# A chunked state recurrence on TensorE: 40 weight columns for the state product, and the state part of u in four 64x64 quarters

## The chip, the cores and the metric

The kernel runs on one core of a Trainium2 chip. The engines named below are PE (TensorE, matrix products; its weight loads are shown as PEld), DVE (VectorE), ACT (ScalarE), POOL (GpSimd) and SP (SyncE, which issues most DMAs). The metric is the time of one execution on the device in microseconds. Three executions of the kernel before took 243.11, 243.59 and 246.12 us; the median is 243.59 us.

## The reference

There are 4 x 8 = 32 heads, 768 time steps and a head width of 40. Each head keeps a 40 x 40 state, and a row of all heads' outputs goes through two dense layers with a squared ReLU between them:

```python
y[:, :, t] = np.einsum('bhd,bhde->bhe', rt, state)
Sa = np.einsum('bhde,bhe->bhd', state, at)
state_decay = state * wt[:, :, None, :] - np.einsum('bhd,bhe->bhde', Sa, bt)
state = state_decay + np.einsum('bhd,bhe->bhde', vt, kt)
...
h = x @ w_in            # x: 3072 x 320, w_in: 320 x 2048
r = np.maximum(h, 0.0)
return (r * r) @ w_out  # w_out: 2048 x 320
```

## The kernel before, in words

Time is cut into 12 chunks of 64 steps. Inside a chunk the recurrence is written as matrix products; the state is carried from chunk to chunk. The 32 heads are 16 pairs (p = 0..7 in each of two groups g = 0, 1; q = 0, 1 is the member of a pair). Heads are stored with 40 numbers in a field of 64, so that a pair fills 128 partitions.

A named step of the plan is a group of instructions on one engine. Those that matter here, for chunk c:

- `AS c` (line 743, PE): the state's part of u, the a rows times the old state. `AR` holds the scaled a for 128 partitions (64 for q = 0, 64 for q = 1); `STb` holds the old state with q = 0 in the upper 64 partitions and q = 1 in the lower 64, each in its own 40 columns and zeros in the other's. One matmul does both heads of a pair: 128 rows, 64 weight columns, 80 moving columns; 16 matmuls, mode "C" (two column halves of the array, by g).
- `EV c` (line 757, PE): adds to the same PSUM tile the part of u from this chunk's v; 32 matmuls of 40 moving columns with masked products `EN` as weights. In chunks 3 to 11 (`EVC`) it has 128 rows and mode "C".
- `u0 c` (ACT or DVE): copies u negated to `NZ`. `NU c` (line 772, PE): 32 matmuls with `EN` as weights and `NZ` moving, mode "Q" (64 rows by 64 columns, two of the four quarters). `u1 c` (ACT or DVE, lines 388 and 385): writes the sum into the `VU` buffer.
- `SC c` (line 793, PE): carries the old state into the new state's PSUM tile, 4 matmuls of 320 columns. `S c g0`, `S c g1` (line 805, PE): adds the products of k and b (`KB`, the weights, 64 columns of which 40 are used) with v and u (`VU`, 40 moving columns); 32 matmuls in a chunk, mode "C". `s c` (line 808, DVE): scales the sum into `STb`.
- `RS c` and `Y c` (PE): the same for the output y, one chunk behind. `EN`, `CX`, `TA`, `TR`, `TK`, `TV`, `TS`, `XT`, `cf`, `ci`: products, transposes and running sums of a chunk, each of many small matmuls. `F`, `FL` and `O`: the dense layers, 128 x 128 weights with 256 or 320 moving columns.

Every matmul has its own weight load, so that PE's program has two instructions for each. All matmuls are issued by a helper at line 402, transposes at 406 and 409.

The order of all instructions on all engines is written out by hand as a text (`ORDER`, lines 87 to 212) and issued as it stands: dense layers of earlier chunks stand between the small groups of later ones. The costs that the steps carry (`d` in `pe`, lines 344 to 349) don't reorder anything when the kernel is built. The class that holds the plan has among its constants:

```python
LAT = {"PE": 235, "ACT": 70, "DVE": 70, "POOL": 80, "SP": 100}
SWITCH = 110
LINE, FETCH = 256, 4350
```

`SC` and `S` are left out in the last chunk, which needs no new state.

Of the kernel before, what the change touches and what calls it, by code (L numbers as in the profile page):

```python
# [7 lines left out]
FP32 = mybir.dt.float32  # L8
# [211 lines left out]
def kernel(  # L220
# [13 lines left out]
    NB, NHH, T, D = r.shape  # L234
# [3 lines left out]
    NJ = NH // 2  # L238
    NP = NJ // 2
# [11 lines left out]
    def rows(g):  # L251
        return slice(64 * g, 64 * g + 64)
# [25 lines left out]
    EVC = range(3, 12)  # L278
# [65 lines left out]
    def pe(name, mode, cols, mms, **kw):  # L344

        d = {"R": max(28.6, cols / 2.4 + 1) / 2, "Q": max(31.0, cols / 2.4 + 1) / 2,
             "C": max(31.0, cols / 2.4 + 1) / 2,
             "D": max(22 if cols < 64 else 60.6, cols / 2.4 + 2.5)}[mode]
        plan.add(name, [("PE", d * len(mms))], ("pe", d, mms), mode=mode, n_mm=len(mms), **kw)
# [51 lines left out]
    def mm(o_, l_, r_, start, stop):  # L401
        return lambda: nc.tensor.matmul(out=o_(), lhsT=l_(), rhs=r_(), start=start, stop=stop,  # L402
                                        skip_group_check=True)
# [320 lines left out]
    def rec(c):  # L724
        KBK = [("KB", c % NK, 0), ("KB", c % NK, 1)]
        q2 = c % 2
        n = NP * D
        kb, vu = KB[c % NK], VU[c % NK]
        VU0 = [("VU0", c % NK, 0), ("VU0", c % NK, 1)]
        hb = ("U", c)  # L730

        def uo(p, g, q, w_=1):
            j = 2 * p + q
            return lambda: slot(hb, FP32)[rows(g), j // NP,
                                          D * (j % NP):D * (j % NP) + D * w_]
        ms = []
        if c > 0:
            for p in range(NP):
                for g in range(2):
                    ms.append(mm(uo(p, g, 0, 2), lambda p=p, g=g: AR[q2][:, 0, g, p, :],  # L740
                                 lambda p=p, g=g: STb[(c - 1) % 2][:, NP * g + p, :, 0:D],
                                 p % 4 == 0, False))
            pe(f"AS {c}", "C", 80, ms, reads=[("AR", q2, 0), ("AR", q2, 1), ("STb", (c - 1) % 2, 0),
                                             ("STb", (c - 1) % 2, 1)],
               writes=[hb], alloc=[hb])
        ms = []
        for p in range(NP):
            for q in range(2):
                for g in range(2):
                    ms.append(mm(uo(p, g, q),  # L750
                                 lambda p=p, q=q, g=g: (EN[q2][:, g, q, p, :] if c in EVC else
                                                        EN[q2][rows(1 - g), g, q, p, :]),
                                 lambda p=p, q=q, g=g: vu[:, NJ * g + 2 * p + q, 0:D]
                                 if c in EVC else vu[rows(1 - g), NJ * g + 2 * p + q, 0:D],
                                 c == 0 and p % 4 == 0 and q == 0, False))
        VU1 = [("VU1", c % NK, 0), ("VU1", c % NK, 1)]
        pe(f"EV {c}", "C" if c in EVC else "Q", 40, ms,
           reads=both(("EN", q2, 0), ("EN", q2, 1)) + VU0 + (VU1 if c in EVC else []),
           writes=[hb], alloc=[hb] if c == 0 else [])
        ew(f"u0 {c}", copy_alts(  # L760
            lambda: NZ[0][:].rearrange("p (s j) e -> p s (j e)", s=2),
            lambda: slot(hb, FP32)[:, :, 0:n], 2 * n, scale=-1.0),
           reads=[hb], writes=[("NZ",)])
        ms = []
        for p in range(NP):
            for q in range(2):
                for g in range(2):
                    ms.append(mm(uo(p, g, q),
                                 lambda p=p, q=q, g=g: EN[q2][rows(g), g, q, p, :],
                                 lambda p=p, q=q, g=g: NZ[0][rows(g), 2 * p + q, :],  # L770
                                 False, True))
        pe(f"NU {c}", "Q", 40, ms, reads=both(("EN", q2, 0), ("EN", q2, 1)) + [("NZ",)],
           writes=[hb])
        for g in range(2):
            ew(f"u1 {c} g{g}", copy_alts(
                lambda g=g: vu[rows(g), NJ * g:NJ * g + NJ, 0:D].rearrange(
                    "p (s j) e -> p s j e", s=2),
                lambda g=g: slot(hb, FP32)[rows(g), :, 0:n].rearrange(
                    "p s (j e) -> p s j e", e=D), 2 * n, scale=-1.0),
               reads=[hb], writes=[("VU1", c % NK, g), ("bank", hb)], free=[hb])  # L780
        if c < NCH - 1:
            hs = ("S", c)
            if c > 0:
                ms = []
                for g in range(2):
                    for q in range(2):
                        ms.append(mm(
                            lambda q=q, g=g: slot(hs, FP32)[rows(q), g, 0:n].rearrange(
                                "p (i e) -> p i e", e=D),
                            lambda q=q: IDQ[:, rows(q)],  # L790
                            lambda q=q, g=g: STb[(c - 1) % 2][:, NP * g:NP * g + NP, q, 0:D],
                            True, False))
                pe(f"SC {c}", "C", n, ms, reads=[("STb", (c - 1) % 2, 0),
                                                ("STb", (c - 1) % 2, 1)],
                   writes=[hs], alloc=[hs])
            for g in range(2):
                ms = []
                for p in range(NP):
                    for q in range(2):
                        ms.append(mm(  # L800
                            lambda p=p, q=q, g=g: slot(hs, FP32)[rows(q), g, D * p:D * p + D],
                            lambda p=p, q=q, g=g: kb[:, NJ * g + 2 * p + q, :],
                            lambda p=p, q=q, g=g: vu[:, NJ * g + 2 * p + q, 0:D],
                            c == 0 and p == 0, True))
                pe(f"S {c} g{g}", "C", 40, ms, reads=KBK + [VU0[g], VU1[g]] + [hs] * g,
                   writes=[hs], alloc=[hs] if c == 0 and g == 0 else [])
            for q in range(2):
                ew(f"s {c} q{q}", [("DVE", c_dve(2 * n), lambda q=q: nc.vector.tensor_tensor(  # L808
                    out=STb[q2][rows(q), :, q, 0:D],
                    in0=slot(hs, FP32)[rows(q), :, 0:n].rearrange("p g (i e) -> p g i e", e=D),  # L810
                    in1=GT[c % NG][rows(q), :, L:L + 1].broadcast_to([64, NJ, D]),
                    op=ALU.mult))],
                   reads=[hs, ("GT", c % NG)], writes=[("STb", q2, q)], free=[hs])
            if c in DTS:
                turn(f"dS {c}", lambda: Sb[q2][:].rearrange("p i q e -> p i (q e)"),
                     lambda: STb[q2][:].rearrange("p i q e -> p (i q e)"),
                     [("STb", q2, 0), ("STb", q2, 1)], [("Sb", q2)])
                return
            ht = ("A", "TS", c)
            ms = []  # L820
            for pi in range(NJ):
                for q in range(2):
                    ms.append(tp(
                        lambda pi=pi, q=q: slot(ht, BF16)[:, q, 64 * pi:64 * pi + 64],
                        lambda pi=pi, q=q: STb[q2][rows(q), pi].rearrange("p x e -> p (x e)"),
                        q))
            if c in WHOLE:
                ms = [tpw(lambda pi=pi, ht=ht: pairs_at(ht, pi),
                          lambda pi=pi: STb[q2][:, pi].rearrange("p x e -> p (x e)"))
                      for pi in range(NJ)]  # L830
            pe(f"TS {c}", *tmode(c), ms, reads=[("STb", q2, 0), ("STb", q2, 1)], writes=[ht],
               alloc=[ht])
            ew(f"tS {c}", copy_alts(
                lambda: Sb[q2][:, :, :, 0:D] if c in WHOLE else Sb[q2][:, :, :, 0:D].rearrange(
                    "p i q e -> p q i e"),
                lambda: (slot(ht, BF16)[:].rearrange("p h (m q e) -> p (h m) q e", q=2, e=64)
                         if c in WHOLE else slot(ht, BF16)[:].rearrange(
                             "p q (i e) -> p q i e", e=64))[:, :, :, 0:D],
                1280, True),
               reads=[ht], writes=[("Sb", q2)], free=[ht])  # L840
# [283 lines left out]
```

## Time and profile before

| | |
|---|---|
| median of three executions | 243.59 us |
| span of the profiled execution, first to last instruction | 241.4 us |
| PE busy | 219.8 us (91%) |
| PE weight loads busy | 173.8 us (72%) |
| DVE, ACT, POOL busy | 185.1, 171.9, 119.3 us |
| matmuls, and as many weight loads | 5360 |

The profiled execution is given by its span alone, without what lies around it; the median is 2.2 us above that span. The page of the profile has the busy time of each engine, the span in 40 slices, the DMA queues, the chain of work that ended last, and the costliest groups of instructions. In a timeline row stand the start, the length, the engine, the line, the operation with its operands and shapes, and the count of instructions merged into the row; a name such as `pb<-STb,AR` is output <- moving operand, weights. Lengths of matmuls are modelled and overlap, so the pace of a group is read from the start of one group to the start of the next.

### The profile page before, as it was taken

Reading aid. Unit: us, or ns where it says so; the run is one execution under the profiler, and the core shown is the slowest. Engines: PE = TensorE matmul, PEld = TensorE weight load, DVE = VectorE, ACT = ScalarE, POOL = GpSimd, SP = SyncE. Lnnn points to the kernel's source line nnn. Section 1 sums busy time; section 2 is a strip of 40 time slices with the busy share of each in tenths; the row PEclk is TensorE's granted clock in tenths of the full one; section 3 lists DMA queues with packets and bytes.
Section 4 is the critical chain, followed back from the end, with each engine's and each line's share of the span. In section 5 each row is a group of like instructions: output and inputs, shape, how many; then the busy total and the mean of one; then the engine's idle time right before and its main releaser. Section 6 shows DMA issues by size and latency. Waiting matters only on the chain.

```text
span 241.4 us, 11825 instructions
## 1 busy us (share of the span) xinstructions
PE 219.8 (91%) x5360; PEld 173.8 (72%) x5360; DVE 185.1 (77%) x237; ACT 171.9 (71%) x225; POOL 119.3 (49%) x117
## 2 busy tenths in 40 slices
PE   0569877999999999999999999999999999999992
PEld 0357666778887787777777877877787777877872
DVE  3779994889988898899789978779888668646430
ACT  3383876879699888976979995975897974572330
POOL 6237816403545572849948379318591750024330
PEclk9967997999999999999999999999999999999998
DMA  6989999997979987888783878978994857093413
GB/s 154 233 185 231 186 217 162 187 203 156 181 158 236 187 163 148 144 194 152 157 169 67 168 178 161 220 157 144 146 188 120 156 106 93 3 161 72 109 24 86
DMA packets 116808, 37.20 MB, mean 154 GB/s; under 512 B 103575, under 2 KB 116375, under 8 KB 116503
## 3 DMA queue, kind: packets, MB, share of 16 engines
q1 hardware_dynamic: 115574, 36.13, 75.7%
q8 instruction: 42, 0.69, 1.2%
q10 hardware_dynamic: 1184, 0.33, 0.6%
q14 instruction: 8, 0.06, 0.1%
HBM read 28.84 MB, written 3.93 MB: 136 GB/s over the span
## 4 chain that ended last, share of the span: by engine, by line
PE 74%; DMA 8%; SPq 7%; DVE 4%; ACT 3%; issue 2%; POOL 1%; POOLq 0%; ACTq 0%
PE pb L402 65%; PE pb L406 6%; DMA G<-in_moe_w_in_dram 4%; PE pb L409 3%; DMA osb<-in_moe_w_out_dram 2%; SPq L433 2%; SPq L1048 2%; DMA raw_w<-in_w_dram 2%; SPq L425 1%; DVE AR L682 1%; POOL WIN L392 1%; SPq L465 1%; DVE VU L385 1%; ACT lnW L548 1%; ACT VU L388 1%
## 5 line engine op out<-in xcount | busy, mean ns | idle before, releaser
L402 PE MATMUL pb<-WOUT,G 128*128 128x320 bf16 (+1 forms) x400 | 57.0, 294 | 0.1
L973 POOL TENSOR_TENSOR G<-G 128x1024 bf16<-128x1024 bf16 x22 | 41.8, 1910 | 28.4 <-ACT G L965 23.4
L402 PE MATMUL pb<-XT,WIN 128*128 128x256 bf16 x384 | 48.3, 273 | 0.0
L402 PEld LDWEIGHTS <-G 128*128 128x128 bf16 x400 | 36.4, 98 | 13.8 <-issue 0.5
L965 ACT ACTIVATE G<-pb 128x1024 bf16<-128x1024 f32 x36 | 36.0, 1021 | 11.1 <-PE pb L402 9.6
L402 PEld LDWEIGHTS <-WIN 128*128 128x128 bf16 x384 | 34.7, 98 | 8.0 <-issue 3.7
L713 DVE TENSOR_TENSOR EN<-pb,MSK 128x1024 bf16<-128x1024 f32 x24 | 28.8, 1216 | 4.9 <-PE pb L402 4.8
L713 DVE TENSOR_TENSOR CX<-pb,MSKI 128x1024 bf16<-128x1024 f32 x24 | 28.7, 1218 | 3.5 <-PE pb L402 3.2
L396 POOL TENSOR_TENSOR KB<-raw_kb,iG 128x640 bf16<-128x640 f32 x10 | 15.8, 1580 | 16.7 <-ACT iG L584 14.9
L808 DVE TENSOR_TENSOR STb<-pb,GT 64x640 bf16<-64x640 f32 x22 | 18.1, 821 | 3.4 <-PE pb L402 3.0
L392 POOL CAST VU<-raw_v 64x640 bf16<-64x640 f32 x17 | 13.3, 785 | 13.3 <-DMA raw_v<-in_v_dram 12.8
L896 DVE TENSOR_TENSOR Yb<-pb,Gin 128x128 bf16<-128x128 f32 (+1 forms) x24 | 12.3, 553 | 9.5 <-PE pb L402 9.4
L590 ACT ACTIVATE Gin<-pb 64x320 f32<-64x320 f32 x36 | 15.4, 428 | 4.6 <-PE pb L402 4.2
L396 POOL TENSOR_TENSOR lo<-lnW,hi 128x640 bf16<-128x640 f32 x7 | 9.8, 1402 | 16.4 <-DVE hi L383 16.2
L402 PE MATMUL pb<-XT,WLAST 64*128 64x256 bf16 x192 | 17.1, 271 | 0.0
L682 DVE TENSOR_TENSOR AR<-pb,GT 128x512 bf16<-128x512 bf16 x24 | 15.9, 683 | 1.6 <-PE pb L406 1.4
L402 PEld LDWEIGHTS <-EN 64*64 64x64 bf16 (+1 forms) x768 | 14.5, 111 | 3.4 <-issue 2.2
L388 ACT ACTIVATE VU<-pb 64x640 bf16<-64x640 f32 x17 | 11.8, 697 | 7.1 <-PE pb L402 4.0
L967 DVE TENSOR_SCALAR G<-pb 128x1024 bf16<-128x1024 f32 x12 | 14.4, 1212 | 1.8 <-PE pb L402 1.8
L388 ACT ACTIVATE VUT<-pb 128x2048 bf16<-128x2048 bf16 x6 | 11.3, 1876 | 5.4 <-PE pb L406 3.1
L402 PE MATMUL pb<-UTI,hi 64*128 64x64 bf16 x192 | 8.2, 198 | 7.3 <-POOL hi L392 6.9
L584 ACT ACTIVATE iG<-pb 128x640 f32<-128x640 f32 x18 | 12.6, 700 | 2.7 <-PE pb L402 2.1
(117 smaller groups left out, 442.7 us busy)
## 6 DMA issues: line engine op xcount, KB each, us to landing
raw_kb<-in_b_dram SPq DMA_DIRECT2D x24, 160.0 KB
raw_kb<-in_k_dram SPq DMA_DIRECT2D x24, 160.0 KB
raw_a<-in_a_dram SPq DMA_DIRECT2D x24, 160.0 KB
raw_v<-in_v_dram SPq DMA_DIRECT2D x24, 160.0 KB
raw_w<-in_w_dram SPq DMA_DIRECT2D x23, 160.0 KB
raw_r<-in_r_dram SPq DMA_DIRECT2D x22, 160.0 KB
out_dram<-osb SPq DMA_DIRECT2D x22, 160.0 KB
osb<-in_moe_w_out_dram SPq DMA_DIRECT2D x8, 320.0 KB
```

Of the source, the lines that this page charges most:

```text
L388: alts.append(("ACT", c_act(n), lambda: nc.scalar.activation(out=o_(), in_=i_(), func=ACTF.Copy, scale=1.0 if scale is None else scale)))
L392: lambda: nc.gpsimd.tensor_copy(out=o_(), in_=i_())))
L396: return [("POOL", 40 + 2.35 * n, lambda: nc.gpsimd.tensor_tensor(out=o_(), in0=a_(), in1=b_(), op=op)), ("DVE", c_dve(n), lambda: nc.vect ...
L402: return lambda: nc.tensor.matmul(out=o_(), lhsT=l_(), rhs=r_(), start=start, stop=stop, skip_group_check=True)
L406: return lambda: nc.tensor.transpose(out=o_(), in_=i_(), identity=IDb[rows(g), :])
L590: nc.scalar.activation(out=Gin[c % NGI][rows(g), NP * jh:NP * jh + NP, :].rearrange("p j e -> p (j e)"), in_=slot(hb, FP32)[rows(g), g, 0: ...
L682: ew(f"tA {c} g{g}", [("DVE", c_dve(512), lambda g=g: nc.vector.tensor_tensor(out=steps(AR[q2][:, 0, g]), in0=turned(ha, g), in1=steps(GT[ ...
L713: evac(f"m{nm} {c} g{g}", lambda s, n: [("DVE", c_dve(n), lambda: nc.vector.tensor_tensor(out=dst[q2][:, g, s].rearrange("p q i t -> p (q ...
L808: ew(f"s {c} q{q}", [("DVE", c_dve(2 * n), lambda q=q: nc.vector.tensor_tensor(out=STb[q2][rows(q), :, q, 0:D], in0=slot(hs, FP32)[rows(q) ...
L965: ("ACT", c_act(1024), lambda gb=gb, hf=hf: nc.scalar.activation(out=gb, in_=slot(hf, FP32)[:], func=ACTF.Relu)),
L967: ("DVE", c_dve(1024), lambda gb=gb, hf=hf: nc.vector.tensor_scalar(out=gb, in0=slot(hf, FP32)[:], scalar1=0.0, scalar2=None, op0=ALU.max))],
L973: ("POOL", 1900, lambda gv=gv: nc.gpsimd.tensor_tensor(out=gv, in0=gv, in1=gv, op=ALU.mult)),
```

## The change

Two edits, both in `rec(c)`; the text of the order stays as it is.

1. `S c` loads 40 weight columns in place of 64 and writes 40 PSUM partitions of each half in place of 64, in chunks 1 to 11 as far as they have the step (1 to 10). Chunk 0, which starts the PSUM tile, keeps 64.
2. In chunks 3 to 11, `AS c` has 32 matmuls in place of 16: each multiplies 64 rows (one q) by 64 weight columns (one g) with 40 moving columns, so that its four kinds use the four 64x64 quarters of the array. The two row halves write two PSUM banks: u's tile has bank q in place of the bank of pair half `j // NP`. `EV`, `NU`, `NZ` and the copy `u1` follow that layout. The mode of the step is "Q" in place of "C"; `EV` stays "C".

PE's program has 10,722 instructions before and 11,010 after: 9 chunks x 16 further matmuls and 16 further weight loads.

```diff
         def uo(p, g, q, w_=1):
+            if c in EVC:
+                return lambda: slot(hb, FP32)[rows(g), q, D * p:D * p + D]
             j = 2 * p + q
...
+        def uz(p, q):
+            return NP * q + p if c in EVC else 2 * p + q
...
-                    ms.append(mm(uo(p, g, 0, 2), lambda p=p, g=g: AR[q2][:, 0, g, p, :],
-                                 lambda p=p, g=g: STb[(c - 1) % 2][:, NP * g + p, :, 0:D],
-                                 p % 4 == 0, False))
-            pe(f"AS {c}", "C", 80, ms, reads=[("AR", q2, 0), ("AR", q2, 1), ("STb", (c - 1) % 2, 0),
+                    if c not in EVC:
+                        ms.append(mm(uo(p, g, 0, 2), lambda p=p, g=g: AR[q2][:, 0, g, p, :],
+                                     lambda p=p, g=g: STb[(c - 1) % 2][:, NP * g + p, :, 0:D],
+                                     p % 4 == 0, False))
+                        continue
+                    for q in range(2):
+                        ms.append(mm(uo(p, g, q), lambda p=p, g=g, q=q: AR[q2][rows(q), 0, g, p, :],
+                                     lambda p=p, g=g, q=q: STb[(c - 1) % 2][
+                                         rows(q), NP * g + p, q, 0:D], p == 0, False))
+            pe(f"AS {c}", *(("Q", 40) if c in EVC else ("C", 80)), ms, reads=[("AR", q2, 0), ("AR", q2, 1), ("STb", (c - 1) % 2, 0),
...
-                                 lambda p=p, q=q, g=g: NZ[0][rows(g), 2 * p + q, :],
+                                 lambda p=p, q=q, g=g: NZ[0][rows(g), uz(p, q), :],
...
-                    "p (s j) e -> p s j e", s=2),
+                    "p (j s) e -> p s j e" if c in EVC else "p (s j) e -> p s j e", s=2),
...
-                            lambda p=p, q=q, g=g: slot(hs, FP32)[rows(q), g, D * p:D * p + D],
-                            lambda p=p, q=q, g=g: kb[:, NJ * g + 2 * p + q, :],
+                            lambda p=p, q=q, g=g: slot(hs, FP32)[
+                                64 * q:64 * q + (D if c else 64), g, D * p:D * p + D],
+                            lambda p=p, q=q, g=g: kb[:, NJ * g + 2 * p + q, 0:D if c else 64],
```

## The prediction

> **What bounds the kernel now.** I read the page first: shares of the engines, the instruction queue and the chain that ended last.
>
> ```profile
> span 241.4 us, 11825 instructions
> PE 219.8 (91%) x5360; PEld 173.8 (72%) x5360; DVE 185.1 (77%) x237; ACT 171.9 (71%) x225; POOL 119.3 (49%) x117
> PE   0569877999999999999999999999999999999992
> q8 instruction: 42, 0.69, 1.2%
> PE 74%; DMA 8%; SPq 7%; DVE 4%; ACT 3%; issue 2%; POOL 1%; POOLq 0%; ACTq 0%
> ```
>
> PE is full from the tenth slice on (about 55 us) and makes up 74% of the chain; before that, loads end last. So PE time is worth its full size in chunks 3 and later, and about nothing before. The queue row matters below: 42 packets, 0.69 MB, 16 KB each. PE's program has 10,722 instructions, which is 42 blocks of 256.
>
> Second, PE's timeline around one chunk, for the pace of a group: start of the group to start of the next.
>
> ```profile
> 105.65 0.48 PE L402 MATMUL pb<-STb,AR 128*64 128x80 bf16 x16
> 105.96 0.66 PE L402 MATMUL pb<-VU,EN 128*64 128x40 bf16 x32
> 106.47 0.46 PE L402 MATMUL pb<-Sb,AR 128*64 128x80 bf16 x16
> 106.75 0.66 PE L402 MATMUL pb<-KB,CX 128*64 128x40 bf16 x32
> 107.35 0.41 PE L406 MATMUL pb<-IDb,tA 64*128 64x64 bf16 x16
> 107.69 0.68 PE L402 MATMUL pb<-NZ,EN 64*64 64x40 bf16 x32
> 108.30 2.35 PE L402 MATMUL pb<-WOUT,G 128*128 128x320 bf16 x16
> ...
> 112.13 0.46 PE L402 MATMUL pb<-STb,IDQ 128*64 128x320 bf16 x4
> 112.43 0.66 PE L402 MATMUL pb<-VU,KB 128*64 128x40 bf16 x32
> 113.02 1.05 PE L402 MATMUL pb<-XT,WIN 128*128 128x256 bf16 x8
> ```
>
> These are AS 5, EV 5, RS 4, Y 4, TA 6, NU 5, O 2, and SC 5, S 5, a dense group. EV, followed by a group of its own shape: 0.51 us for 32, 15.9 ns each. RS: 0.28 for 16. Y, the twin of EV but followed by another array shape: 0.60. So a change of shape costs 0.09 us. NU has 0.61 = 0.51 + 0.10: two quarters at 15.9 ns, and a change. AS takes 0.31, S 0.59 = 0.50 + 0.09.
>
> Third, where PE stops although it waits for no engine.
>
> ```profile
> 172.44 0.25 PE L402 MATMUL pb<-KB,CX 128*64 128x40 bf16 x5
> 172.85 0.59 PE L402 MATMUL pb<-KB,CX 128*64 128x40 bf16 x27 [0.17 <-issue]
> 173.38 1.05 PE L402 MATMUL pb<-XT,WIN 128*128 128x256 bf16 x8
> ...
> 202.05 0.64 PE L402 MATMUL pb<-AR,KBT 64*128 64x64 bf16 x31
> 203.10 0.19 PE L402 MATMUL pb<-AR,KBT 64*128 64x64 bf16 x1 [0.41 <-issue]
> ```
>
> Both stops fall inside a group. The first group needs 0.94 us to its successor instead of Y's 0.60: 0.34 lost. In the second, 31 of 32 matmuls take 1.05 us; at two for some 30 ns they need 0.48: 0.57 lost. Together 0.9 us. What lies between stops is shown by the windows (length, then PE busy and matmuls, PEld busy and weight loads, DVE, ACT, POOL):
>
> ```profile
> 32.28:37.93 5.65, 3.67 (x128) 3.41 (x128) 3.77 (x4) 4.93 (x7) 1.83 (x2) 1.00 1.06 246
> 106.78:172.85 66.07, 65.76 (x1801) 50.80 (x1796) 56.84 (x72) 51.63 (x71) 44.57 (x34) 1.00 0.81 154
> 167.81:172.85 5.04, 4.88 (x137) 3.53 (x134) 4.78 (x6) 3.73 (x8) 2.90 (x3) 1.00 1.12 106
> 172.85:203.10 30.25, 29.76 (x767) 23.46 (x767) 22.55 (x28) 24.11 (x34) 15.05 (x13) 1.00 0.79 149
> 199.04:203.10 4.06, 3.65 (x140) 2.92 (x135) 3.20 (x5) 1.10 (x3) 0.00 (x0) 1.00 1.14 134
> 65.82:70.01 4.19, 4.19 (x138) 3.60 (x134) 3.78 (x7) 3.78 (x7) 2.29 (x2) 1.00 0.63 118
> 172.85:177.16 4.31, 4.31 (x128) 3.46 (x128) 2.58 (x5) 3.61 (x7) 3.09 (x3) 1.00 0.97 203
> ```
>
> 32.28 and 37.93 are two earlier stops: exactly 128 + 128 = 256 instructions apart. 172.85 and 203.10 are 1534 counted instructions apart, six blocks of 256 with two that aren't counted. **The stops sit at block boundaries: PE waits for its next 256 instructions.** One block seems to be fetched while the one before it runs, so a block can't pass faster than a fetch. Stalled blocks took 4.06, 5.04 and 5.65 us; the one of 4.06 holds only 3.49 of work. The shortest unstalled ones here are 4.19 and 4.31. (A window cut in full flow also counts a dozen instructions still running.) I take 3.8 us as the floor of a block: between 3.49, which was too short, and 4.06, where one was held; the ends I keep are 3.4 and 4.06, with 5.0 for a single slow fetch.
>
> **The change part by part.**
>
> *S with 40 weight columns.* S runs at EV's 15.9 ns a matmul, RS with twice the moving columns at 17.5, so the 64-column weight load sets the pace of S, not its 40 moving columns. Bounds: nothing gained (15.9), or half of RS's pace for 80 columns (8.8). In proportion to columns it would be 9.9; I take 12, since small matmuls show no pace near that: 32 x 3.9 ns = 0.12 us a chunk. Eight of the ten chunks (3 to 10) lie where PE is full: **-1.0 us**, ends 0 and -1.8.
> [...]
>
> *AS in four quarters.* 32 matmuls. If each quarter keeps the 31.8 ns a matmul of EV and NU, four at once take 8 ns each: 0.25, and 0.03 for starting after another shape (AS 0.31 against RS 0.28). EV behind it keeps mode "C", so a change of shape is new: 0.09. That makes 0.37 against 0.31, x 9 chunks = **+0.5 us**. The trace shows no group with four quarters. Ends: 4.6 ns each, if only moving columns counted (-0.3 us), and 15.9, if four are no faster than NU's two: 0.61 against 0.31, +2.7 us.
>
> *Layout of u, NZ, VU.*
>
> ```profile
> L388 ACT ACTIVATE VU<-pb 64x640 bf16<-64x640 f32 x17 | 11.8, 697 | 7.1 <-PE pb L402 4.0
> ```
>
> The same counts and sizes on PE, ACT and DVE; the copy u1 writes runs of 40 as before. I cost it at nothing. It is covered by the dense groups that stand between NU and S; without that cover 5% of a copy of 0.7 us in 9 chunks would be 0.3 us.
>
> *Block boundaries.* Each quartered AS adds 32 instructions, so from chunk 3 on every boundary falls 32, 64, 96... instructions earlier in the same order. The boundary of 106.78 (14 blocks before 172.85) stands two matmuls into Y 4; after AS 3, 4 and 5 it stands 96 instructions earlier: 2 matmuls of Y, 16 of RS, 30 of EV, that is at 105.99. I carried all boundaries over in this way. Most new blocks need over 4 us. These, in the old times, don't (with the long block ahead of the third):
>
> ```profile
> 86.58:90.07 3.49, 3.49 (x121) 3.09 (x120) 3.10 (x5) 3.20 (x6) 2.69 (x3) 1.00 0.97 185
> 105.99:108.58 2.59, 2.59 (x138) 2.40 (x133) 2.41 (x5) 1.38 (x3) 2.05 (x2) 1.00 0.90 167
> 112.90:119.31 6.41, 6.41 (x133) 4.51 (x128) 6.33 (x7) 5.58 (x6) 6.14 (x6) 1.00 0.74 145
> 119.31:121.39 2.08, 2.08 (x126) 2.05 (x125) 0.50 (x2) 2.00 (x3) 2.08 (x2) 1.00 1.05 181
> 135.91:139.29 3.38, 3.38 (x126) 2.77 (x118) 2.80 (x4) 3.31 (x5) 1.01 (x2) 1.00 0.76 145
> 155.05:158.82 3.77, 3.77 (x134) 3.01 (x130) 2.96 (x4) 2.96 (x5) 0.00 (x0) 1.00 0.82 187
> ```
>
> The second is EV 5 to NU 5, 256 instructions with no dense matmul but three. The one from 119.31 is most of AS 6, RS 5, EV 6, Y 5 and cf 7. The block 199.04:203.10 stays where it is, with 3.49 of work, less 0.12 by S 10. Against 3.8 us they lack 0.3 + 1.2 + 1.7 + 0.4 + 0.0 + 0.4 = **+4.0 us** of new stops. The old two are gone or counted in: **-0.9 us**. Nothing hides a stop: PE is full after 55 us, with hardly a wait to take it back from. Floors of 3.4 and 4.06 give 1.6 and 5.9; a fetch of 5 us in one of the other blocks adds up to 1.
>
> *Sum:* -1.0 + 0.5 + 4.0 - 0.9 = +2.6: span 241.4 to 244.0; by the same step the median goes from 243.59 to **246.2 us** (+1.1%).
>
> **The rivals.**
>
> 1. *Fetches keep up.* If more than one block is held ahead, or a fetch begins earlier when dense matmuls stand queued, short blocks pass after long ones, as they do here (the 2.08 block follows one of 6.41). Then 243.59 - 1.0 + 0.5 - 0.9 + about 1 for what remains = 243.2; with both products at their best ends and no stop left, 240.6. Against it: the block of 3.49 that ends at 203.10 was held. [...] The 0.17 and 0.41 us of "issue" above speak against it in this trace.
> 2. *Slower by over 2%: the quarters don't run four at a time.* NU's two quarters go at exactly the pace of two column halves; if that pace is the issue of load and matmul pairs rather than the loads in a quarter, AS costs 0.61. The place is AS in nine chunks, the price +2.7 instead of +0.5. Its blocks then last 0.24 longer, so at a floor of 3.8 the stops are 3.4: 247.8. At 4.06 they are 5.0: 249.4. It passes 248.5 from a floor of about 3.9. For it: no faster pair than this stands in the rows above. Against it: a pair of RS moves 80 columns in 35 ns while another runs beside it, so the halves do overlap.
> 3. *The narrow load gains nothing*, as 40 columns still occupy a 64-column half: S stays at 0.59, 1.0 more than the forecast: 247.2.
>
> **How the numbers follow.** Forecast 246.2: 0.50. Fetches keep up (243.2): 0.24. Quarters at NU's pace (247.8 to 249.4): 0.16. No gain in S (247.2): 0.10. A measurement of this kernel can tell about 2% from no change: 238.7 to 248.5. The forecast with its ends goes from 243.8 (floor 3.4) to 248.1 (floor 4.06), and slow single fetches can carry it over 248.5; with the second rival that is 0.19 for slower. Faster by over 2% needs more than all gains together: 0.01. Within 2%: 0.80. The range 242.9 to 249.3 leaves out half of the first rival's lower part and the upper tail.
>
> **What would show it.** S 5 from its first row to the dense group: 0.47 instead of 0.59. AS: 64*64 64x40 x32, EV 0.37 behind it. New "issue" stops of over 1 us inside the dense group behind NU 5 and inside cf 7 (the UTI products behind Y 5), each 256 instructions from a neighbour. No stops there would mean the first rival; an EV 0.6 behind AS the second. I would be wrong altogether if DVE or ACT became the end of the chain around u1 and s.

## The result and the profile after

Four executions of the changed kernel took 250.55 to 252.95 us, median 251.53; four of the kernel before, on the same chip, 243.11 to 247.62, median 244.86. The ratio is **1.034 [1.029, 1.040]**: slower, by three times the forecast. It is taken over undisturbed executions alone, so it doesn't equal the quotient of the two medians.

The page of the changed kernel (its third row is PE's busy tenths in 40 slices, its fourth the granted clock):

```profile
span 249.8 us, 12113 instructions
PE 221.4 (89%) x5504; PEld 173.1 (69%) x5504; DVE 186.8 (75%) x237; ACT 172.3 (69%) x225; POOL 118.6 (47%) x117
PE   0568968989999999988699998999999999999993
PEclk9999999999999999999959999999999999999999
q8 instruction: 43, 0.70, 1.2%
PE 72%; DVE 8%; SPq 8%; issue 4%; DMA 4%; ACT 2%; DVEq 0%; ACTq 0%
```

The span grew by 8.4 us, PE's busy time by 1.6 only. "Issue", time in which an engine waits for nothing that the profile shows, has gone from 2% of the chain to 4%. PE's row has a 6 and the clock's row a 5 near the middle, where before both were full. One more instruction packet was moved, 43 for 42, as 288 more instructions, a little over one block, should need. PE's waits in the changed kernel (us in total, times, longest):

```profile
PE pb L402 <- issue: 8.4, 9, 2.6
```

Now the chunk that the prediction showed, on PE's timeline of the changed kernel:

```profile
104.56 0.43 PE L402 MATMUL pb<-STb,AR 64*64 64x40 bf16 x32
104.93 0.69 PE L402 MATMUL pb<-VU,EN 128*64 128x40 bf16 x32
105.45 0.46 PE L402 MATMUL pb<-Sb,AR 128*64 128x80 bf16 x16
...
106.68 0.68 PE L402 MATMUL pb<-NZ,EN 64*64 64x40 bf16 x32
107.29 0.58 PE L402 MATMUL pb<-WOUT,G 128*128 128x320 bf16 x3
109.05 1.94 PE L402 MATMUL pb<-WOUT,G 128*128 128x320 bf16 x13 [1.18 <-issue]
...
114.15 0.20 PE L402 MATMUL pb<-VU,KB 128*40 128x40 bf16 x1 [0.81 <-issue]
...
125.40 0.23 PE L402 MATMUL pb<-UTI,lo 64*128 64x64 bf16 x1 [2.56 <-issue]
...
127.07 4.45 PE L402 MATMUL pb<-WOUT,G 128*128 128x320 bf16 x16
131.45 0.47 PE L406 MATMUL pb<-IDb,tA 64*128 64x64 bf16 x16
```

What to see, from the start of one group to the start of the next: AS, now 64x64 quarters, takes 0.37 us, EV behind it 0.52. S with 40 columns, where no stop falls into it, takes 0.49 (S 6) where it took 0.59. There are stops behind NU 5, after the third of 16 dense matmuls (109.05); one matmul ahead of the end of S 5 (114.15); and in cf 7 (125.40). Behind the last one, 16 dense matmuls take 4.38 us (127.07 to 131.45); in the prediction's rows the same number took under 2.4. The windows between stops (length, PE busy and matmuls, PEld busy and loads, DVE, ACT, POOL, granted clock, DMA share, GB/s):

```profile
85.34:88.91 3.57, 3.57 (x138) 3.13 (x137) 3.10 (x5) 3.21 (x6) 2.73 (x3) 1.00 0.85 142
104.98:109.05 4.07, 2.89 (x135) 2.41 (x132) 3.89 (x8) 1.43 (x4) 3.54 (x3) 1.00 0.92 193
109.05:114.15 5.10, 4.29 (x129) 3.32 (x129) 2.90 (x4) 3.32 (x5) 5.02 (x4) 1.00 0.88 140
120.54:125.39 4.85, 2.30 (x143) 2.11 (x139) 1.21 (x3) 2.02 (x3) 4.79 (x5) 0.94 0.65 104
125.39:131.60 6.21, 6.20 (x59) 3.53 (x61) 3.47 (x5) 2.98 (x5) 0.84 (x2) 0.50 0.01 3
138.77:143.36 4.59, 4.26 (x136) 3.35 (x132) 4.29 (x5) 4.03 (x5) 2.50 (x2) 1.00 0.87 178
143.36:147.37 4.01, 3.60 (x128) 2.74 (x129) 3.19 (x4) 3.67 (x7) 1.60 (x2) 1.00 0.79 167
163.88:168.21 4.33, 3.93 (x150) 3.07 (x138) 3.42 (x5) 3.57 (x6) 0.00 (x0) 1.00 0.77 144
208.18:211.84 3.66, 3.54 (x139) 2.79 (x133) 2.81 (x5) 1.09 (x2) 0.00 (x0) 1.00 1.23 140
```

All but the fifth are one block of 256 instructions. Seven of the eight were held at their end and took 3.66 to 5.10 us; the first passed in 3.57 without a stop. The fifth is the stretch behind the long stop, at **half the clock**.

Setting each matmul that is the same in both programs beside its twin gives where the 8.4 us came from (start after minus start before; the steps of that difference from one matmul to the next):

| place in the changed kernel | us |
|---|---|
| ahead of 60 us | -1.2 |
| stops at 109.05, 114.15, 125.40 | +1.34, +0.99, +2.75 |
| half clock to 131.6 | +2.8 |
| stops at 143.36, 147.37, 168.21 | +0.50, +0.56, +0.57 |
| PE waits for `STb` at 155.52 | +0.97 |
| the old stop in Y gone; that of 0.57 in chunk 10 now 0.28 | -0.35, -0.29 |
| the products themselves and small waits, all chunks | about +0.1 |
| behind the last matmul | -0.4 |

The first row isn't the change's doing: that stretch waits for loads, and a kernel described below whose program for PE is the same as before up to there (the one that splits AS in its old mode) is 1.4 us ahead at the same place.

### The profile page after: what moved, and what is told of

The parts are those of the page before. It is cut to its first block, busy times and chain, and to the rows that moved or that the text cites. A ratio compares the mean times of both kernels' runs of the same rounds, so it can differ in the third digit from the quotient of the medians.

```text
span 249.8 us, 12113 instructions
## 1 busy us (share of the span) xinstructions
PE 221.4 (89%) x5504; PEld 173.1 (69%) x5504; DVE 186.8 (75%) x237; ACT 172.3 (69%) x225; POOL 118.6 (47%) x117
## 4 chain that ended last, share of the span: by engine, by line
PE 72%; DVE 8%; SPq 8%; issue 4%; DMA 4%; ACT 2%; DVEq 0%; ACTq 0%
PE pb L402 63%; PE pb L406 5%; SPq L1060 4%; PE pb L409 3%; SPq L433 2%; DMA CX<-in_moe_w_in_dram 2%; DMA raw_w<-in_w_dram 2%; DVE STb L820 1%; DVE lo L398 1%; DVE CX L713 1%; DVE KBT L528 1%; SPq L425 1%; DVE AR L682 1%; DVE EN L713 1%; DVE VU L385 1%
## 5 line engine op out<-in xcount | busy, mean ns | idle before, releaser
L402 PE MATMUL pb<-WOUT,G 128*128 128x320 bf16 (+1 forms) x400 | 59.3, 301 | 1.3 <-issue 1.2
L985 POOL TENSOR_TENSOR G<-G 128x1024 bf16<-128x1024 bf16 x22 | 42.4, 1937 | 30.5 <-ACT G L977 25.6
L402 PEld LDWEIGHTS <-G 128*128 128x128 bf16 x400 | 37.1, 100 | 16.5 <-issue 2.3
L908 DVE TENSOR_TENSOR Yb<-pb,Gin 128x128 bf16<-128x128 f32 (+1 forms) x24 | 12.3, 553 | 9.7 <-PE pb L402 9.6
L633 POOL MEMSET VU<- 64x1024 bf16 x13 | 12.3, 946 | 11.2 <-PE pb L402 10.2
L392 POOL CAST VU<-raw_v 64x640 bf16<-64x640 f32 x17 | 12.2, 716 | 9.4 <-DMA raw_v<-in_v_dram 8.8
```

The source lines that it names most:

```text
L985: ("POOL", 1900, lambda gv=gv: nc.gpsimd.tensor_tensor(out=gv, in0=gv, in1=gv, op=ALU.mult)),
```

## The experiments

The theory: PE waits for its program at block boundaries, so the loss follows the number and the place of instructions. Against it stood: the quarters or their layout cost the time; a part of it is the S edit's; the program's place at the start or the end doesn't matter.

**The two edits apart.** First only the `S` lines of the diff:

```diff
-                            lambda p=p, q=q, g=g: slot(hs, FP32)[rows(q), g, D * p:D * p + D],
-                            lambda p=p, q=q, g=g: kb[:, NJ * g + 2 * p + q, :],
+                            lambda p=p, q=q, g=g: slot(hs, FP32)[
+                                64 * q:64 * q + (D if c else 64), g, D * p:D * p + D],
+                            lambda p=p, q=q, g=g: kb[:, NJ * g + 2 * p + q, 0:D if c else 64],
```

> Only the 40-column state product; AS, EV and u's layout as before, PE's program again 10,722 instructions. Theory (PE waits for its next block of 256 instructions, and only the instruction count moves the boundaries): the boundaries fall on the same instructions as before, S costs 0.49 in place of 0.59 us, eight chunks count, so 0.8 us less than before, within half a us for the two old stops. Rival (the narrow load itself brings what was lost in the full change): slower than before by several us.

Measured: 0.998 [0.993, 1.003], median 241.05 us beside 242.39. S 5 on its timeline of PE:

```profile
110.26 0.56 PE L402 MATMUL pb<-VU,KB 128*40 128x40 bf16 x32
110.76 1.05 PE L402 MATMUL pb<-XT,WIN 128*128 128x256 bf16 x8
```

0.50 us to the dense group, where it was 0.59. The product gains what the trace of the changed kernel shows, and no large stop comes with it: this edit doesn't change the number of instructions. Behind 60 us PE loses 0.37 us at one boundary (113.82) where the kernel before lost nothing, and the two old stops of 0.34 and 0.57 us are all but gone, so which of the short blocks are held isn't the same in every execution.

Then everything but those lines (against the changed kernel):

```diff
-                            lambda p=p, q=q, g=g: slot(hs, FP32)[
-                                64 * q:64 * q + (D if c else 64), g, D * p:D * p + D],
-                            lambda p=p, q=q, g=g: kb[:, NJ * g + 2 * p + q, 0:D if c else 64],
+                            lambda p=p, q=q, g=g: slot(hs, FP32)[rows(q), g, D * p:D * p + D],
+                            lambda p=p, q=q, g=g: kb[:, NJ * g + 2 * p + q, :],
```

> Only AS in quarters with its layout; S with 64 columns as before. Theory of the blocks: the boundaries move as in the full change and the stops stand at the same instructions; 0.8 us more than the full change, that is 8 to 9 us more than before, with a stop of over 2 us behind Y 5 and PE's clock at half for some us after it. Rival (the two edits together are needed for the loss): close to before plus 0.7 us.

Measured: 1.021 [1.004, 1.037], median 248.09: slower, but by some 5 us and not the 8 to 9 that were expected. Its timeline of PE has the two large stops at the same instructions, and no slow stretch behind them:

```profile
110.22 1.94 PE L402 MATMUL pb<-WOUT,G 128*128 128x320 bf16 x13 [1.46 <-issue]
...
124.81 0.20 PE L402 MATMUL pb<-UTI,lo 64*128 64x64 bf16 x1 [1.71 <-issue]
...
125.83 2.35 PE L402 MATMUL pb<-WOUT,G 128*128 128x320 bf16 x16
128.11 0.41 PE L406 MATMUL pb<-IDb,tA 64*128 64x64 bf16 x16
```

The 16 dense matmuls take 2.28 us here. So the loss comes with the quartered AS, and the half clock isn't a fixed part of it.

**The same instructions without quarters.** The kernel before, with AS in 32 matmuls of one head each, 128 rows, mode "C", the old banks and the old layout:

```diff
+                    for q in range(2) if c in EVC else ():
+                        ms.append(mm(uo(p, g, q), lambda p=p, g=g: AR[q2][:, 0, g, p, :],
+                                     lambda p=p, g=g, q=q: STb[(c - 1) % 2][:, NP * g + p, q, 0:D],
+                                     p % 4 == 0 and q == 0, False))
+                    if c in EVC:
+                        continue
```

> AS in chunks 3 to 11 as 32 matmuls of 40 columns, but in the old mode (128 rows by 64 columns), with the old layout and banks of u; S as before. No quarters, no new bank, no added change of shape; the same 288 added instructions as in the full change. Theory of the blocks: AS 0.51 in place of 0.31 us in nine chunks gives 1.8 us, and stops as in the full change 6 to 7 us more, in all 7 to 10 us slower than before. Rival (the quarters, the banks or the new layout make the loss): 1.8 us slower than before and no more.

Measured: 1.019 [1.006, 1.031], median 247.35. Its stops, on PE's timeline, and the window behind the second (columns as above):

```profile
109.87 1.94 PE L402 MATMUL pb<-WOUT,G 128*128 128x320 bf16 x13 [1.53 <-issue]
...
125.12 0.20 PE L402 MATMUL pb<-UTI,lo 64*128 64x64 bf16 x1 [1.86 <-issue]
...
126.14 3.92 PE L402 MATMUL pb<-WOUT,G 128*128 128x320 bf16 x16
```

```profile
125.12:131.00 5.88, 5.88 (x117) 3.76 (x117) 3.91 (x6) 3.03 (x6) 1.38 (x2) 0.71 0.01 3
```

The two large stops stand at the very matmuls where the changed kernel has them. Nothing of the quarters, the second bank or the layout is in this kernel; 288 further instructions are. So the stops need none of the quarters. The times alone would not show it: of the 4.5 us of the ratio (7 to 10 were expected), 2.0 are the slower AS itself, 0.53 us instead of 0.31 in nine chunks, and with the interval what is left could be nothing. It is the trace that has the stops.

**The count put back.** The changed kernel once more, and beside it the changed kernel without the low part's 16 matmuls of `cf` in chunks 3 to 11 (the running sum then lacks its correction), so that each chunk has as many instructions as before the change:

```diff
-            for x in (h_, l_):
+            for x in ((h_, l_) if c < 3 else (h_,)):
...
-                        lambda g=g: UTI[rows(g), 0:L], x is h_ and p == 0, x is l_))
+                        lambda g=g: UTI[rows(g), 0:L], x is h_ and p == 0, x is l_ or c >= 3))
```

> The changed kernel once more, beside the next two on one chip. Expected 3 to 9 us above the kernel before: stops of 1 to 3 us behind NU 5 and behind Y 5, some of 0.3 to 0.9 us elsewhere, and some us more where PE's clock falls to half after a stop.

> The changed kernel without the products of the low part in cf in chunks 3 to 11 (the running sum of the log decay then lacks its correction): 16 matmuls and 16 weight loads fewer in each chunk, as many as AS has more, so that the block boundaries come back to within 64 instructions of those before. The work left out costs 16 x 14.5 ns in nine chunks, 2.1 us. Theory of the blocks: the stops go with it; product terms -0.8 (S) + 0.7 (AS and EV) - 2.1, about one us of stops as before: 2 to 3 us less than the kernel before. Rival (the quarters, their banks or the clock make the loss by themselves): the changed kernel's time less 2.1 us, 1 to 7 us more than before.

Measured: the changed kernel 1.026 [1.020, 1.033], median 248.66; with the count put back 0.989 [0.984, 0.994], median 240.66. The work left out is 9 x 16 matmuls at about 15 ns, 2.1 us; the time fell by 8.0 (medians). This is the clearest run for the theory, as the quarters and all else of the change are in both. PE's timeline of the one with the low part:

```profile
108.23 1.94 PE L402 MATMUL pb<-WOUT,G 128*128 128x320 bf16 x13 [0.63 <-issue]
123.68 0.20 PE L402 MATMUL pb<-UTI,lo 64*128 64x64 bf16 x1 [2.49 <-issue]
```

and of the one without it, with its clock row and its waits:

```profile
107.22 2.35 PE L402 MATMUL pb<-WOUT,G 128*128 128x320 bf16 x16
```

```profile
PEclk9967997999999999999999999999999999999999
...
PE pb L402 <- issue: 1.0, 2, 0.7
```

The quarters are still there, and behind NU 5 the dense matmuls run on without a stop; behind 60 us one stop of 0.41 is left, and no half clock. So some 6 of the 8 us are stops and what follows them. This kernel is ahead of the kernel before only because it leaves work out. In the second execution of the changed kernel the block that the first held to 4.07 us took 3.53, and the one ending near 88 us, which the first passed without a stop, lost 0.6.

**The same work, boundaries moved.** The kernel before with 52 tiny matmuls (64 rows, 128 weight columns, 16 moving columns; 104 instructions with their loads) put at the very start, while PE waits for its first loads:

```diff
-ORDER = """SP ldw 0; SP ldb 0; SP ldk 0; POOL zv 1; POOL zr 0; SP ldk 1; ACT ln 0; SP ldb 1; POOL hi 0; ACT
+ORDER = """PE3 WR26; SP ldw 0; SP ldb 0; SP ldk 0; POOL zv 1; POOL zr 0; SP ldk 1; ACT ln 0; SP ldb 1; POOL hi 0; ACT
...
+            for h in range(2):
+                nc.tensor.matmul(out=t[:, h, 0:16], lhsT=UTI[rows(h), :], rhs=UTI[rows(h), 0:16],
+                                 start=True, stop=True, skip_group_check=True)
```

(`WR26` asks the helper `fill` for 26 times these two matmuls; the next kernels use the same helper.)

> The kernel before with 52 tiny matmuls (16 columns, 104 instructions) at the very start of PE's program, while PE waits for the first loads; nothing else is changed, all later work and its order is that of before. Theory of the blocks: every boundary falls 104 instructions earlier; by the old trace nine blocks after 60 us then need under 3.7 us, two of them 2.3, which at 4.2 us a block is 10 us of stops, so 7 to 13 us slower than before. Rival (stops come from what the AS groups do): no change, since 52 tiny matmuls at the start lie in waiting time.

Measured: 1.014 [1.002, 1.026], median 246.32. A stop of its PE timeline, in NU 5:

```profile
107.40 0.68 PE L402 MATMUL pb<-NZ,EN 64*64 64x40 bf16 x31
109.61 0.20 PE L402 MATMUL pb<-NZ,EN 64*64 64x40 bf16 x1 [1.53 <-issue]
```

New stops at new places, and half clock from 109.9 to 113.3. In this trace, whose execution was the longest of the four (249.11 us), the kernel is 0.7 us ahead of the one before at 60 us and 6.4 behind at its last matmul, though all work after the padding is the same. By the ratio the loss is some 3.4 us, far below the 7 to 13 that were expected; four blocks with 3.3 to 3.5 us of work passed unstalled. So the same order with its boundaries elsewhere is slower, but not every short block is held.

**Padding to gain.** Could a shift of the boundaries help the kernel with S alone? 216 instructions at the start of it:

```diff
-ORDER = """SP ldw 0; SP ldb 0; SP ldk 0; POOL zv 1; POOL zr 0; SP ldk 1; ACT ln 0; SP ldb 1; POOL hi 0; ACT
+ORDER = """PE3 WR54; SP ldw 0; SP ldb 0; SP ldk 0; POOL zv 1; POOL zr 0; SP ldk 1; ACT ln 0; SP ldb 1; POOL hi 0; ACT
```

> 40 weight columns in S and 108 tiny matmuls (216 instructions) at the start of PE's program, where PE waits for loads. By the old trace every block after 55 us then has over 4.2 us of work. Theory of the blocks: 0.5 to 1 us less than with the 40 columns alone, 1.3 to 1.8 us less than before, with no stop over 0.4 us after 58 us. Rival: as the 40 columns alone, or slower by the time of the padding, up to 2 us.

Measured: 1.001 [0.995, 1.006], median 243.1. Behind 60 us no boundary stop is left, as meant; but at 54 us this kernel is already 3 us behind the one with S alone, with a longer stop on the way (PE's timeline):

```profile
40.20 0.61 PE L402 MATMUL pb<-AR,KBT 64*128 64x64 bf16 x15 [1.72 <-issue]
```

Behind 60 us it gains 0.4 on that one. So the padding gained nothing; that it is what cost the head its 3 us isn't shown, as two executions of the kernel with S alone differ by 1.6 there themselves.

**The fetch by itself.** The kernel before with 1024 tiny matmuls behind its end, when few transfers are left, and with the same at its start, among the first loads:

```diff
-OB 11 u2; DVE oc 11; PE OB 11 u3; ACT ob 11; ACT st1 11 g0; SP st0 11 g0"""
+OB 11 u2; DVE oc 11; PE OB 11 u3; ACT ob 11; ACT st1 11 g0; SP st0 11 g0; PE3
+WR512"""
```

> The kernel before with 1024 tiny matmuls (2048 instructions, eight blocks) behind its last matmul, while hardly any DMA is left. A block of them is about 1.8 us of work. It measures the floor of a block by itself: if one block is fetched ahead, a stop every 256 instructions and blocks of 3.3 to 4.1 us each; if several blocks are held ahead, the first few pass at 1.8 us.

```diff
-ORDER = """SP ldw 0; SP ldb 0; SP ldk 0; POOL zv 1; POOL zr 0; SP ldk 1; ACT ln 0; SP ldb 1; POOL hi 0; ACT
+ORDER = """PE3 WR512; SP ldw 0; SP ldb 0; SP ldk 0; POOL zv 1; POOL zr 0; SP ldk 1; ACT ln 0; SP ldb 1; POOL hi 0; ACT
```

> The same 1024 tiny matmuls at the very start of PE's program, while the first loads keep the DMA engines full. Theory of the blocks: stops every 256 instructions; if the floor depends on DMA traffic, blocks while the DMA engines are over 0.9 busy take 4 to 6 us, and those with little traffic 3.3 to 4. If traffic doesn't matter, all take the same as at the end.

PE's timeline with the tiny matmuls at the end:

```profile
238.75 1.88 PE L1085 MATMUL pb<-UTI 64*128 64x16 bf16 x128 [1.59 <-issue]
242.21 1.88 PE L1085 MATMUL pb<-UTI 64*128 64x16 bf16 x128 [1.57 <-issue]
...
249.39 1.88 PE L1085 MATMUL pb<-UTI 64*128 64x16 bf16 x128 [1.85 <-issue]
```

and windows from stop to stop with them at the start (columns as above):

```profile
9.22:14.05 4.83, 1.88 (x129) 1.79 (x128) 0.23 (x1) 0.00 (x0) 0.00 (x0) 1.00 0.88 202
...
18.60:22.05 3.45, 1.87 (x128) 1.78 (x128) 0.00 (x0) 0.00 (x0) 0.00 (x0) 1.00 0.74 167
22.05:26.33 4.28, 1.88 (x128) 1.78 (x128) 0.00 (x0) 0.00 (x0) 0.00 (x0) 1.00 0.25 77
26.33:29.78 3.45, 1.88 (x128) 1.79 (x128) 0.00 (x0) 0.00 (x0) 0.00 (x0) 1.00 0.02 5
```

Every 128 matmuls, 256 instructions, PE stops, with 1.88 us of work done. The executions took 264.37 and 266.3 us beside 242 to 243 for the kernel before. A block takes 3.45 to 3.73 us with the DMA engines all but idle (share 0.02) and up to 4.83 with them at 0.88, though not in step with their share: 3.45 at 0.74, 4.28 at 0.25.

**The fetch in the traces.** The traces also hold the packets of the instruction queue (q8 on the page), 16,384 bytes each, about one for each block. Put beside the seven held blocks of the changed kernel they show what a stop waits for (us; the start of a block is found by counting 256 instructions back, to about 0.1 us):

| PE goes on at | block's start to packet's start | packet | packet's end to PE going on |
|---|---|---|---|
| 109.05 | 1.63 | 0.88 | 1.56 |
| 114.15 | 2.57 | 0.88 | 1.66 |
| 125.40 | 1.90 | 1.43 | 1.53 |
| 143.36 | 1.74 | 1.27 | 1.59 |
| 147.37 | 1.73 | 0.94 | 1.33 |
| 168.21 | 1.94 | 0.93 | 1.47 |
| 211.84 | 1.41 | 0.92 | 1.34 |

In 46 held blocks of eight traces PE went on 1.27 to 1.80 us after a packet had landed, and the packet took 0.88 to 1.73. The part that varies most is the first, the time until the packet starts: 0.5 to 2.8 us. It is short where a short block passes: 0.54 us in 85.34:88.91 above, and 0.2 to 0.7 in four blocks of 3.3 to 3.5 us that passed behind 60 us in the padded kernel before. The two held blocks with 0.5 and 0.7 took only 3.5 us.

**S alone once more:**

> The 40 columns alone once more, in five rounds, since its first interval reached over no change. S is 0.10 us shorter in the eight chunks that count and no instruction is added: 0.8 us less than before, a ratio of 0.997. If the spread of the block fetches is larger than that, the interval will still hold 1.

Measured: 0.999 [0.995, 1.003], median 241.69 beside 242.15. The 0.7 us that its trace shows in the eight groups S are not resolved by the times. No version tried is shown to be ahead of the kernel before with all its work.

## Why the prediction was wrong

By its steps:

- **PE is worth its full size from 55 us on: right.** The difference between the two programs grows from there by what PE lost, and the stops are not taken back. Of the small gains of S, waits a few us later swallow up to 0.1 us in three chunks.
- **S, -1.0 us: right.** It took 0.10 us less, 0.49 to 0.52 for 0.59 to 0.62, in six of the eight chunks (in chunk 5 as the kernel with S alone shows it), 0.06 less in chunk 4 and nothing less in chunk 3, where the group behind it starts no sooner: -0.7.
- **AS, +0.5: right.** 0.37, as forecast; EV behind it 0.52 instead of 0.51. The four quarters run at once: 32 matmuls in 0.37 with a change of shape, against 0.61 had they gone at NU's pace. The second rival falls, and the third with S.
- **The layout of u, at nothing: right** as far as the timeline shows; the kernel that splits AS without it has the same large stops.
- **The places of the stops: right for the two that were named,** behind NU 5 and in cf 7, each over 1 us, and the mechanism, a block that passes no faster than its fetch, is shown by the kernels that keep the count or move the boundaries alone, and by the packets. The first rival, that fetches keep up, falls: it left about 1 us for stops, and the new ones alone were 7.0.
- **"I take 3.8 us as the floor of a block": this step failed.** The term, +4.0 us of new stops, measured 7.0 (1.34 + 0.99 + 2.75 + 0.50 + 0.56 + 0.57 + 0.28). There is no one floor: a block of tiny matmuls took 3.45 to 4.83, and the held ones here 3.66 to 5.10. Of the blocks that were listed, five lost 5.5 instead of 4.0 for all, and the one ending at 88.91 lost nothing. Two that weren't listed, with 4.1 us of work each, lost 1.5 more. The allowance for one slow fetch, "adds up to 1", was too small for a quantity that spreads by 1.4 us from block to block. The sums for the two ends were also off: by the lengths listed there a floor of 3.4 gives 2.2 and not 1.6, one of 4.06 gives 5.7 and not 5.9; neither reaches what was measured.
- **"Nothing hides a stop" was half of it: a stop can also cost more than its length.** At half clock the stretch behind 125.40 lost 2.8 us. That term wasn't in the sum. It was in the trace of before, though, in its clock row and at one of the stops that the prediction itself used (page, PE's timeline, window):

```profile
PEclk9967997999999999999999999999999999999998
```

```profile
37.93 0.60 PE L402 MATMUL pb<-KB,CX 128*64 128x40 bf16 x19 [1.07 <-issue]
```

```profile
37.93:41.50 3.57, 3.57 (x61) 3.06 (x63) 2.15 (x3) 1.26 (x2) 2.22 (x3) 0.53 0.92 133
```

- **0.97 us at 155.52 was not in the sum.** The prediction named it only as a sign of being wrong (DVE at the end of the chain around s). PE's transposes wait there for `STb` (0.81 us idle on the timeline), which DVE writes late, behind its step `lo`. DVE and POOL of the changed kernel:

```profile
151.59 2.18 DVE L398 TENSOR_TENSOR lo<-lnW,hi 128x640 bf16<-128x640 f32 x1
```

```profile
151.56 1.54 POOL L396 TENSOR_TENSOR KB<-raw_kb,iG 128x640 bf16<-128x640 f32 x1
```

and of the kernel before, where POOL's `KB` began 1.5 us later than `lo`:

```profile
143.61 0.81 DVE L398 TENSOR_TENSOR lo<-lnW,hi 128x640 bf16<-128x640 f32 x1
```

```profile
145.09 1.54 POOL L396 TENSOR_TENSOR KB<-raw_kb,iG 128x640 bf16<-128x640 f32 x1
```

In the changed kernel the two steps began within 0.03 us; the stops ahead of them may have moved the engines against each other. In the second execution of the changed kernel the same happened (148.57 on DVE, 2.18 us; 148.53 on POOL). No run took this overlap away alone, so that it is the cause is read from the timelines, not shown by an experiment.

With the measured sizes the sum is -0.7 (S) + 0.5 (AS) + 0.1 (EV behind another shape) + 7.0 (new stops) - 0.9 (old ones) + 2.8 (half clock) + 1.0 (the wait for `STb`) = +9.8, less 1.2 ahead of 60 us and 0.4 behind the last matmul: 8.2 against the 8.4 of the spans.

**Open:** what lets the packet of one block start after 0.2 us and that of another after 2.8 (the DMA share alone doesn't tell), and whether S alone gains its 0.3%.

## What to carry to other kernels

When PE's program is long and PE is full, count instructions and not only time: splitting a group in two for a better use of the array can be nearly free in the group (here 0.06 us a chunk) and dear a few microseconds later (here 7.0 us of new stops), where a stretch of small matmuls no longer covers the fetch of the next 256 instructions. Before such an edit, cut the old trace into blocks at the new boundaries, price each block with the whole spread of fetches seen, 3.45 to 5.65 us here, and not with one middle value, and look at the clock row behind every stop. An edit that keeps the count, such as a narrower weight load, keeps the boundaries where they were.

## What the runs showed that was not expected

**The clock's change follows a period of 3.4 us.** In the traces of the kernels before and after, half clock lasts 3.41 us (38.14 to 41.56, before) or 6.83 (14.25 to 21.08, before; 124.80 to 131.62, after), except at the end, where little work is left. The full stretches that the traces hold whole are 17.07 and 197.97 us (before), 105.81 and 119.47 us (after): like the halves, whole multiples of 3.413 us. PE's idle time in the period just before seems to decide whether full clock falls (periods of 3.41 us counted on from the changes of the clock in each trace). In the full stretch behind 60 us, periods with 1.04 to 1.31 us idle (five of them, four kernels; 1.18 in the changed kernel's 107.73 to 111.14) were followed by full clock, those with 1.53, 1.82, 1.96 and 2.49 (four executions; 1.96 in the changed kernel's 121.38 to 124.80) by half. So the stop of 1.71 us at 124.81 in the kernel without the S edit cost no clock, as a period ended within it, and one of 1.53 in the padded kernel before did. Ahead of 60 us and at the very end the line is not so clean: in the changed kernel a period with 1.40 us idle (36.05 to 39.46) and one with 1.83 (244.26 to 247.68) were followed by full clock. At half clock, the period from 124.80, with 0.60 us idle, was followed by a second half one, and that from 128.21, with none idle, by full clock.

**Two vector steps took longer when they overlapped.** POOL's product at line 396 and DVE's at line 398, both with two inputs in SBUF, took 1.54 and 0.81 us apart. Begun together, DVE's took 2.18; begun 0.78 us apart, in the kernel with the count put back, DVE's 1.37 and POOL's 1.99:

```profile
142.21 1.37 DVE L398 TENSOR_TENSOR lo<-lnW,hi 128x640 bf16<-128x640 f32 x1
```

```profile
142.99 1.99 POOL L396 TENSOR_TENSOR KB<-raw_kb,iG 128x640 bf16<-128x640 f32 x1
```

The 2.18 us are a little less than the two lengths one after the other (1.54 + 0.81 = 2.35), and POOL's step kept its 1.54 there. With DVE first both were lengthened, DVE's by 0.56 and POOL's by 0.45. What the two steps share is not shown by any run.

**Small matmuls share the array well:** from start to start 8.2 ns each with four quarters (AS, 0.25 us from the first to the last of 32), against 16.2 in the kernel that splits AS over two column halves, and 12.3 ns over two column halves with 40 weight columns (S) instead of 15.3 with 64.
